# A new hand-written order for a recurrent attention layer with an MLP behind it, and its first weight loaded in three parts

## The chip, the cores and the metric

The kernel runs on one core of a Trainium2 chip. The time is the device time of one execution in microseconds (us): the median of three runs, of one core. A core has five engines that run side by side, each through its own instructions in their order: TensorE (PE in the profile; its weight loads are PEld), VectorE (DVE), ScalarE (ACT), GpSimd (POOL) and SyncE (SP), which here only issues transfers. Transfers run on 16 DMA engines. An instruction starts when those ahead of it on its engine and those whose results it needs are done.

## The reference

Four batches of eight heads, 768 steps, 48 numbers to a head. A state of 48x48 to a batch and head is carried from step to step, and its output goes through a two-layer MLP with a piecewise activation:

```python
for t in range(S):
    cur = einsum('bhd,bhe->bhde', u[None] * kt, vt)
    y[:, :, t] = einsum('bhd,bhde->bhe', rt, state + cur)
    state = w[None, :, :, None] * state + einsum('bhd,bhe->bhde', kt, vt)
x = y.transpose(0, 2, 1, 3).reshape(3072, 384)
h = x @ w_in                        # w_in: 384 x 2048
g = where(h >= 1, h, where(h <= -1, 0, (h + 1)**2 / 4))
out = g @ w_out                     # w_out: 2048 x 384
```

## The kernel before

**Tiles.** The 768 steps are cut into 6 chunks of 128, the 4 batches into 2 pairs. One chunk of one pair is a *group* g = 0 to 11 (g = 2 x chunk + pair); one chunk of one batch is a *unit* n = 2g or 2g+1. In a chunk the recurrence becomes matrix products: K and R are scaled by powers of w (`Ks`, `Rs`), turned (`T` and `TT` on TensorE for groups 0 to 2, `KRT`, a transposing transfer, from group 3 on), multiplied (`A`) and masked (`AT`); `Sp` is the chunk's addition to the state, `Tm`, `decay` and `sbf` carry the state on, `Y` is the output of a unit. The term with u goes beside it: `KU`, `RKU`, `usum` make one number to a row and head, `V2` multiplies V with it, and `y` adds that to `Y`. `X` and `xT` turn y: by TensorE and a copy for groups 0 to 2, by a transposing transfer (`xT` on SP's queue, tile `xT<-yy`) from group 3 on; `xT.8` is the one for group 4. V itself is cast to bf16 in step `V` (from tile `VF`).

**The MLP.** For group g and quarter q of the 2048 columns, `mm1.g.q` makes 512 columns of h for 256 rows (12 matmuls, line 526; in group 0 the first two quarters go in two halves), `relu` and `square` on ScalarE and `gate` on VectorE make the activation, and `mm2.g.j.q` (line 554, 4 matmuls) adds a quarter to the output of unit j. `o` copies it out of PSUM, `out` stores it. PSUM has three large buffers (h0 to h2), shared by `T`, `A` and the results of `mm1`, and two small banks.

**Weights.** `w_in` and `w_out` are loaded from f32 to bf16 by transfers that GpSimd issues (lines 290 and 294), in parts: `w_in.i`, `w_out.i`. Part i of `w_out` holds quarter i.

**The order.** It is written out by hand: `ORDER` is a list of steps, and each engine gets its instructions in the order of that list. A step is `name.numbers:buffers@engine`; `@D`, `@P`, `@A` put it on VectorE, GpSimd or ScalarE. `~k` puts k products of zeros ahead of a step, and `warm.k` is k of them (lines 204 and 608): they compute nothing. [...]

Of the kernel before, what the change touches and what calls it, by code (L numbers as in the profile page):

```python
# [14 lines left out]
P = 128  # L15
# [8 lines left out]
W_IN = 2  # L24
# [11 lines left out]
warm.18 load.K.0.0:0 load.R.0.0:0 load.K.0.1 load.R.0.1 load.K.1.0:1 load.R.1.0:1 bcu:0 u_bc@D KU.0.0@P:0 RKU.0.0@P:0  # L36
lw loadV.0.0:0 bcw:1 load.K.1.1 KU.0.1@D loadV.0.1 wcol:0 Wdn_p:0 Ks.0.0@D:0 Wup_p load.R.1.1 Rs.0.0@D:0 wCm
KU.1.0@P:1 loadV.1.0:1 Ks.1.0@D:1 warm.4.h.2 T.0:1 load.K.2.0:2 Wdn RKU.1.0@P:1 Rs.1.0@D:1 Rs.0.1@D V.0.0@A:0
RKU.0.1@P T.2:2~3 TT.0@A:0 usum.0.0@D:0 Ks.1.1@D Ks.0.1@D KU.1.1@P Wup Sp.0:0 TT.2@D:1 A.0:1 V.0.1@A load.R.2.0:2
AT.0.1:0 RKU.1.1@P Tm.0@D Sp.1:1~5 T.1:2 Tm.1@D w_in.0 V.1.0@A:1 A.2:1 Rs.1.1@D loadV.1.1 Sp.2:0 AT.0.0 TT.1@D:2  # L40
usum.1.0@A:1 A.1:0~8 V2.0.0@P:0 Ks.2.0@P:2 AT.2.0:1 loadV.2.0:0 V2.1.0@A:1 Y.0:1 T.3:2 sbf.0@A Tm.2@D usum.0.1@D Y.2:0
TT.3@D:3 y.2:0 AT.1.1:2 Rs.2.0@P:2 A.3:1~14 X.2:0 V2.0.1@A y.0:1 AT.3.0:3 warm.2.h.2 X.0:1 T.5:2~8 AT.1.0 xT.2@A:0
T.4:0 TT.5@D:0 Y.1:0 w_in.1 load.K.3.0:0 xT.0@A:1 sbf.1@A usum.1.1@D A.5:1 mm1.0.0.0:2 KU.2.0@P:0 y.1:2 TT.4@D:1
load.R.3.0:0 V.1.1@A X.1:1 Y.3:0 AT.5.0:0 A.4:0 V2.1.1@P xT.1@A mm1.0.0.1 V.2.0@A:2 Sp.5:1 y.3:0 RKU.2.0@P:0
relu.0.0:0 X.3:0 Tm.5@D:0 mm1.0.1.0:1 AT.4.0:1 xT.3@A decay.5 square.0.0:0 usum.2.0@D:0 Sp.4:1 mm1.0.1.1 w_out.0 Y.4:0
relu.0.1:1 mm1.1.1.-1:0 gate.0.0:0 square.0.1:1 Tm.4@D:1 mm1.0.2.-1:2 relu.1.1:0 Y.5:1 square.1.1:0 V2.2.0@P:0 w_out.1
y.4:1 gate.0.1:1 w_out.2 X.4:0 w_out.3 mm1.0.3.-1:1 xT.4@A:2 gate.1.1:2 relu.0.2:1 Sp.3:0 y.5:2 mm1.1.0.-1:0
# [56 lines left out]
def kernel(  # L104
# [33 lines left out]
    def flat(x):  # L138
# [24 lines left out]
        out=umask, in_=umask, compare_op=ALU.is_ge, fill=1.0,  # L163
# [486 lines left out]
```

## Time and profile before

| | |
|---|---|
| runs | 175.46, 175.96, 178.86 us; median 175.96 |
| profiled execution | span 176.4 us; the page gives no other time of it |
| busy in it | PE 165.0, ACT 135.2, DVE 130.3, POOL 120.2 us |
| granted clock of TensorE over the span | 0.987 |
| products of zeros | 24 (line 608) and 38 (line 204) |

Idle time of an engine costs only where something late waits for it. A busy PE is not PE at its peak; TensorE's own rate is seen in the durations of single steps and in the granted clock (PEclk, 1.00 is full).

### The profile page before, as it was taken

How to read it: one execution, taken by the hardware profiler on the slowest of the kernel's cores; microseconds unless marked ns; L12 is line 12 of the kernel's file. 1: busy time of each engine (PE TensorE's matmuls, PEld its weight loads, DVE VectorE, ACT ScalarE, POOL GpSimd, SP SyncE). 2: the span in 40 equal slices, each digit the busy share in tenths (PEclk: the TensorE clock that was granted, in tenths of full speed). 3: DMA queues.
4: the chain of work that ended last, by engine and by line, in shares of the span. 5: the costliest groups of instructions: out<-in, count | busy, mean ns of one | idle time of the engine just before them, and what ended most of it. 6: DMA issues, size and time to landing. Idle time of an engine off the chain costs nothing.

```text
span 176.4 us, 4159 instructions
## 1 busy us (share of the span) xinstructions
PE 165.0 (94%) x1684; PEld 125.2 (71%) x1684; DVE 130.3 (74%) x167; ACT 135.2 (77%) x194; POOL 120.2 (68%) x97
## 2 busy tenths in 40 slices
PE   6998699999999999779999999999999999999992
PEld 5776587766787766458686777885878767777671
DVE  5599779857987578727978889788895877461471
ACT  4399879996987995319989697989399994888540
POOL 6699999990899999999399799999349400000000
PEclk9999999999999999969999999999999999999998
DMA  5999999999999999996999997989982400312022
GB/s 109 221 219 192 216 175 234 207 165 209 238 172 196 191 202 252 158 183 175 196 221 211 185 183 159 266 149 243 194 197 93 89 17 4 97 37 89 4 89 89
DMA packets 106967, 28.78 MB, mean 163 GB/s; under 512 B 100930, under 2 KB 106180, under 8 KB 106948
## 3 DMA queue, kind: packets, MB, share of 16 engines
q1 hardware_dynamic: 103888, 25.24, 73.6%
q0 software_dynamic: 2912, 3.15, 11.4%
q8 instruction: 13, 0.21, 0.5%
q10 hardware_dynamic: 148, 0.13, 0.2%
q14 instruction: 6, 0.05, 0.1%
HBM read 20.45 MB, written 4.72 MB: 143 GB/s over the span
## 4 chain that ended last, share of the span: by engine, by line
PE 71%; DMA 13%; DVE 7%; ACT 5%; POOL 1%; issue 1%; DVEq 0%; POOLq 0%
PE hp L526 31%; PE op L554 30%; DMA VF<-in_v_dram 5%; DMA w_out_sb<-in_moe_w_out_dram 4%; DMA xT<-yy 3%; DVE AT L421 3%; PE A L406 2%; PE Y L446 2%; PE Y L441 2%; PE Sp L432 1%; ACT V L212 1%; PE ub L242 1%; POOL V L369 1%; PE wb L237 1%; ACT RKU L355 1%; DVE yy L468 1%
## 5 line engine op out<-in xcount | busy, mean ns | idle before, releaser
L526 PE MATMUL hp<-xT,w_in_sb 128*128 128x256 bf16 (+1 forms) x600 | 72.0, 271 | 3.4 <-DMA xT<-yy 2.2
L554 PE MATMUL op<-w_out_sb,gt 128*128 128x384 bf16 (+2 forms) x400 | 71.9, 320 | 0.1
L544 DVE SCALAR_TENSOR_TENSOR gt<-sq,hp 128x1024 bf16<-128x1024 f32 x48 | 57.9, 1216 | 16.2 <-ACT sq L539 16.1
L526 PEld LDWEIGHTS <-w_in_sb 128*128 128x128 bf16 x600 | 56.2, 99 | 13.9 <-issue 3.1
L534 ACT ACTIVATE pt<-hp 128x1024 f32<-128x1024 f32 x48 | 48.7, 1018 | 17.7 <-PE hp L526 17.4
L539 ACT ACTIVATE sq<-pt 128x1024 f32<-128x1024 f32 x48 | 50.4, 1057 | 1.2
L554 PEld LDWEIGHTS <-gt 128*128 128x128 bf16 x400 | 36.5, 98 | 19.3 <-issue 0.5
L421 DVE TENSOR_TENSOR AT<-A,umask 128x1024 bf16<-128x1024 f32 x22 | 26.5, 1218 | 2.2 <-PE A L406 1.9
L337 POOL TENSOR_TENSOR KU<-K,u_bc 128x768 f32<-128x768 f32 (+1 forms) x13 | 21.6, 1658 | 2.0 <-DVE u_bc L212 2.0
L344 POOL TENSOR_TENSOR RKU<-R,KU 128x768 f32<-128x768 f32 (+1 forms) x14 | 22.2, 1589 | 0.3
L489 POOL TENSOR_TENSOR state<-Tm,wCm 128x384 f32<-128x384 f32 x16 | 16.0, 1003 | 8.8 <-DVE Tm L476 8.6
L369 POOL TENSOR_TENSOR V<-V,diag 128x768 f32<-128x768 bf16 (+1 forms) x12 | 16.4, 1365 | 7.1 <-ACT V L212 4.7
L327 POOL TENSOR_TENSOR Ks<-Wdn,K 128x768 bf16<-128x768 f32 x10 | 18.2, 1818 | 1.2 <-DMA K<-in_k_dram 1.2
L327 POOL TENSOR_TENSOR Rs<-Wup,R 128x768 bf16<-128x768 f32 x10 | 18.2, 1819 | 0.1
L476 DVE TENSOR_TENSOR Tm<-Sp,state 128x384 f32<-128x384 f32 x16 | 8.9, 555 | 7.3 <-POOL Ks L327 3.4
L468 DVE TENSOR_TENSOR yy<-Y,V 128x384 bf16<-128x384 f32 x18 | 9.9, 554 | 5.0 <-PE Y L446 3.5
L212 ACT CAST V<-VF 128x768 bf16<-128x768 f32 (+1 forms) x14 | 10.2, 737 | 3.6 <-DMA VF<-in_v_dram 3.5
L446 PE MATMUL Y<-V,AT 128*128 128x48 bf16 x192 | 11.4, 185 | 1.2 <-POOL AT L416 0.9
L446 PEld LDWEIGHTS <-AT 128*128 128x128 bf16 x192 | 9.8, 98 | 2.8 <-POOL AT L416 1.3
L357 DVE TENSOR_REDUCE diag<-RKU 128x16 f32<-128x768 f32 (+1 forms) x13 | 11.1, 852 | 0.9 <-POOL RKU L344 0.9
L212 ACT COPY oo<-op 128x384 f32<-128x384 f32 x13 | 6.2, 476 | 6.7 <-PE op L554 6.3
L212 ACT CAST state_bf<-state 128x384 bf16<-128x384 f32 x20 | 10.0, 503 | 0.0
(77 smaller groups left out, 127.2 us busy)
## 6 DMA issues: line engine op xcount, KB each, us to landing
out_dram<-oo SPq DMA_DIRECT2D x11, 384.0 KB, 3.7
K<-in_k_dram SPq DMA_DIRECT2D x10, 384.0 KB, 4.8
R<-in_r_dram SPq DMA_DIRECT2D x10, 384.0 KB, 4.9
VF<-in_v_dram SPq DMA_DIRECT2D x10, 384.0 KB, 5.8
w_in_sb<-in_moe_w_in_dram POOLq DMA_DIRECT2D x2, 768.0 KB, 8.6
w_out_sb<-in_moe_w_out_dram POOLq DMA_DIRECT2D x4, 384.0 KB, 7.5
K<-in_k_dram SPq DMA_DIRECT2D x4, 192.0 KB, 3.8
R<-in_r_dram SPq DMA_DIRECT2D x4, 192.0 KB, 3.7
```

The costliest lines, as they stand in the source:

```text
L212: nc.scalar.copy(out, in_) if e == "A" else engines[e].tensor_copy(out, in_)
L327: engines[e].tensor_mul(of_unit(dst, j0, j1)[:, :, :, :D], rep(tab, j1 - j0), of_unit(tiles[what, g], j0, j1))
L337: engines[e].tensor_mul(of_unit(tiles["KU", g], j0, j1), of_unit(tiles["K", g], j0, j1), rep(u_bc, j1 - j0))
L344: engines[e].tensor_mul(of_unit(tiles["RKU", g], j0, j1), of_unit(tiles["R", g], j0, j1), of_unit(tiles["KU", g], j0, j1))
L369: engines[e].tensor_mul(tiles["V2", g][:, hs, :], tiles["V", g][:, hs, :], tiles["diag", g][:, hs].unsqueeze(2).to_broadcast([P, hs.stop - ...
L421: nc.vector.tensor_mul(t.rearrange("p i n t -> p (i n) t"), tiles.pop(("A", n)).rearrange("p i n t -> p (i n) t"), umask.unsqueeze(1).to_b ...
L446: nc.tensor.matmul(t[:, 2 * p + i, :], tiles["AT", n][:, i, p, :], tiles["V", g][:, j * H + 2 * p + i, :], start=(c == 0), stop=True, skip ...
L526: nc.tensor.matmul(hp[:, f, cols], w_in_sb[:, i, n0 : n0 + P], tiles["xT", g][:, units, i, :], start=(i == 0), stop=(i == nK - 1), skip_gr ...
L534: nc.scalar.activation(tiles["pt", g, q], tiles["hp", g, q], AF.Relu, bias=0.5, scale=0.5)
L539: nc.scalar.activation(tiles["sq", g, q], tiles.pop(("pt", g, q)), AF.Square, bias=0.0)
L544: nc.vector.scalar_tensor_tensor(out=gt, in0=tiles.pop(("sq", g, q)), scalar=1.0, in1=tiles.pop(("hp", g, q)), op0=ALU.min, op1=ALU.max)
L554: nc.tensor.matmul(t, tiles["gt", g, q][:, f, j * P : (j + 1) * P], w_out_sb[:, n, cols], start=(n == 0), stop=(n == nF - 1),)
```

## The change

`w_in` comes in three parts: columns 0 to 511 (quarter 0), 512 to 1023 (quarter 1) and 1024 to 2047 (quarters 2 and 3). The order is another one throughout, with the same computation. Of the steps with a free choice of engine, VectorE takes 3 more of `KU`, 6 more of `RKU`, 1 of `Ks`, 2 of `Rs`, 6 of `V`, 8 of `sbf`, 3 of `xT`, one of `usum` and one of `V2`, and gives up 4 of `TT`, 4 of `o` and `u_bc`. GpSimd loses what VectorE gains of `KU`, `RKU`, `Ks`, `Rs`; two whole-group `V2` go from GpSimd to ScalarE. The products of zeros go from 62 to 42.

```diff
-W_IN = 2
+W_IN = (0, 512, 1024, 2048)
...
-warm.18 load.K.0.0:0 load.R.0.0:0 load.K.0.1 load.R.0.1 load.K.1.0:1 load.R.1.0:1 bcu:0 u_bc@D KU.0.0@P:0 RKU.0.0@P:0
+load.K.1.0:1 loadV.1.0:1 lw warm.2.h.2 bcw:1 bcu:0 V.1.0@A:4 Wdn_p:2 load.K.0.0:0 load.R.0.0:0 Wup_p Wup u_bc@A
...
     def w_in_go(e, bk, i):
-        n = slice(i * DF // W_IN, (i + 1) * DF // W_IN)
+        n = slice(W_IN[i], W_IN[i + 1])
         nc.gpsimd.dma_start(out=w_in_sb[:, :, n], in_=w_in_src[:, :, n])
```

**GpSimd, from its first `KU` to the second part of w_in.** Before (`V_327<-V,diag` is a half `V2`; `AT<-AT` is the mask of a first unit; x384 is half a group, 16x48 or 768 a whole one):

```order
L337 TENSOR_TENSOR KU<-K,u_bc 128x384
L344 TENSOR_TENSOR RKU<-R,KU 128x384
L290 DMA w_in_sb<-in_moe_w_in_dram 128x3x1024
L416 AFFINE_SELECT AT<-AT 128x1024
L369 TENSOR_TENSOR V_327<-V,diag 128x384
L327 TENSOR_TENSOR Ks<-Wdn,K 128x16x48
L327 TENSOR_TENSOR Rs<-Wup,R 128x16x48
L416 AFFINE_SELECT AT<-AT 128x1024
L290 DMA w_in_sb<-in_moe_w_in_dram 128x3x1024
```

After:

```order
L369 TENSOR_TENSOR V_239<-V,diag 128x384
L369 TENSOR_TENSOR V_274<-V,diag 128x384
L416 AFFINE_SELECT AT<-AT 128x1024
L344 TENSOR_TENSOR RKU<-R,KU 128x384
L290 DMA w_in_sb<-in_moe_w_in_dram 128x3x512
L327 TENSOR_TENSOR Rs<-Wup,R 128x16x48
L290 DMA w_in_sb<-in_moe_w_in_dram 128x3x512
L416 AFFINE_SELECT AT<-AT 128x1024
L290 DMA w_in_sb<-in_moe_w_in_dram 128x3x1024
L294 DMA w_out_sb<-in_moe_w_out_dram 128x4x384
```

Ahead of the first part of w_in stood seven halves of `KU` and `RKU`, now five (the rows shown begin behind the first four of them); two half `V2` and a mask have moved ahead of it, and the first part of w_out follows right behind the last part of w_in.

**SP, the transfers ahead of `xT.8`** (the row `xT<-yy`; KT and RT are `KRT`, `out_dram<-oo` is `out`). Before:

```order
L304 DMA VF<-in_v_dram 128x16x48
L304 DMA R<-in_r_dram 128x16x48
L304 DMA VF<-in_v_dram 128x16x48
L398 DMA_TRANSPOSE RT<-Rs 128x8x128
L587 DMA out_dram<-oo 128x2x384
L304 DMA K<-in_k_dram 128x16x48
L511 DMA_TRANSPOSE xT<-yy 128x6x128
```

After:

```order
L398 DMA_TRANSPOSE KT<-Ks 128x8x128 x2
L398 DMA_TRANSPOSE RT<-Rs 128x8x128
L304 DMA R<-in_r_dram 128x16x48
L304 DMA VF<-in_v_dram 128x16x48
L304 DMA K<-in_k_dram 128x16x48
L511 DMA_TRANSPOSE xT<-yy 128x6x128
```

A store and a transpose no longer stand among the four transfers ahead of it.

**VectorE, the gates of groups 2 and 3** (`gt<-sq,hp` is `gate`, `diag<-RKU` is `usum`, `yy<-Y` is `y`). Before:

```order
L544 SCALAR_TENSOR_TENSOR gt<-sq,hp 128x1024 x2
L212 COPY oo<-op 128x384
L544 SCALAR_TENSOR_TENSOR gt<-sq,hp 128x1024 x2
L357 TENSOR_REDUCE diag<-RKU 128x16
L544 SCALAR_TENSOR_TENSOR gt<-sq,hp 128x1024 x2
L421 TENSOR_TENSOR AT<-A,umask 128x1024 x2
```

After:

```order
L544 SCALAR_TENSOR_TENSOR gt<-sq,hp 128x1024
L337 TENSOR_TENSOR KU<-K,u_bc 128x768 x2
L544 SCALAR_TENSOR_TENSOR gt<-sq,hp 128x1024
L344 TENSOR_TENSOR RKU<-R,KU 128x768
L544 SCALAR_TENSOR_TENSOR gt<-sq,hp 128x1024
L212 CAST V<-VF 128x768
L357 TENSOR_REDUCE diag<-RKU 128x16
L544 SCALAR_TENSOR_TENSOR gt<-sq,hp 128x1024
L327 TENSOR_TENSOR Rs<-Wup,R 128x16x48
```

Between the gates now stand `KU.4`, `KU.5`, `RKU.4`, `V.4` and `Rs.5`, which were GpSimd's and ScalarE's, and which need loads of K, R and V.

On TensorE the steps from `mm1.0.2` (the first that needs columns from 1024 on) up to `mm1.4.0` (the first that needs `xT.8`) are the same set in both kernels but for `Y.5`, which now stands ahead of `mm1.0.2`. Behind the second `Y` of group 4 there were a quarter of `mm2`, two `A` and four more quarters with two `Sp` among them; now there are two `A`, four quarters and two `Sp`.

126 lines of the change are left out of this document (63 added, 63 removed).

## The prediction

> **What bounds the kernel now.** I read the engines' shares first, then the span by stretches, then the chain that ended last. The shares:
>
> ```profile
> PE 165.0 (94%) x1684; PEld 125.2 (71%) x1684; DVE 130.3 (74%) x167; ACT 135.2 (77%) x194; POOL 120.2 (68%) x97
> DMA  5999999999999999996999997989982400312022
> ```
>
> TensorE leads by 30 us, and the DMA engines are full for the first three quarters of the span. Where TensorE is not full shows in the stretches (busy us of PE, PEld, DVE, ACT, POOL, then PEclk, DMA share, GB/s):
>
> ```profile
> 22.00:31.00 9.00, 8.15 (x129) 7.08 (x130) 7.80 (x10) 7.75 (x10) 8.68 (x9) 1.00 1.19 205
> 31.00:64.00 33.00, 32.84 (x296) 24.71 (x292) 24.51 (x28) 29.30 (x37) 28.04 (x20) 1.00 1.20 196
> 64.00:76.00 12.00, 9.61 (x106) 5.87 (x105) 10.05 (x12) 5.74 (x9) 11.55 (x9) 1.00 1.24 193
> 76.00:80.00 4.00, 3.94 (x33) 3.15 (x33) 0.79 (x2) 1.15 (x2) 4.00 (x3) 0.57 1.08 212
> 80.00:100.00 20.00, 19.61 (x212) 15.03 (x210) 17.00 (x20) 18.04 (x21) 16.03 (x11) 1.00 0.95 203
> 100.00:160.00 60.00, 60.00 (x615) 45.93 (x613) 46.99 (x52) 49.19 (x59) 33.08 (x22) 1.00 0.62 131
> ```
>
> From 31 on TensorE works without a gap but for one hole, 64 to 76, and runs at a clock of 0.57 for 4 us behind it. Another order can win there at most the 2.4 us idle in that stretch, 4 x (1 - 0.57) = 1.7 us of clock, and 0.39 us idle in 80 to 100: 4.5 us. All else must come from the head, before 31. The chain names what both wait for:
>
> ```profile
> 14.46 9.60 DMA VF<-in_v_dram
> 30.26 7.92 DMA w_out_sb<-in_moe_w_out_dram
> 69.89 6.13 DMA xT<-yy
> 76.06 2.72 PE hp L526 x12
> ```
>
> In the head these are transfers of V and of the weights; in the hole it is `xT.8`, which landed 6.1 us after its issue. TensorE's own rows at the two places (start, duration, in brackets the idle time before):
>
> ```profile
> 29.18 1.48 PE L526 MATMUL hp<-xT,w_in_sb 128*128 128x256 bf16 x12 [0.29 <-DMA w_in_sb<-in_moe_w_in_dram]
> 73.07 0.81 PE L554 MATMUL op<-w_out_sb,gt 128*128 128x384 bf16 x4
> 76.06 2.72 PE L526 MATMUL hp<-xT,w_in_sb 128*128 128x256 bf16 x12 [2.18 <-DMA xT<-yy]
> 79.54 1.47 PE L526 MATMUL hp<-xT,w_in_sb 128*128 128x256 bf16 x12
> ```
>
> `mm1.0.2` starts at 29.18, when the second half of w_in lands. The last quarter of group 3 ends at 73.88, and `mm1.4.0` starts at 76.06, at half speed (2.72 us; 1.47 at 79.54). Between those two steps TensorE hardly pauses, so a delay of `mm1.0.2` is carried to 73.88 whole.
>
> **The change, part by part. First the weights.** When does GpSimd issue them?
>
> ```profile
> 3.55 1.62 PE L242 MATMUL ub<-u_row,ones 97*128 97x384 f32 x2 [0.40 <-DVE wCm L179]
> 13.26 0.93 POOL L290 DMA_DIRECT2D w_in_sb<-in_moe_w_in_dram  x1
> 26.91 0.80 POOL L294 DMA_DIRECT2D w_out_sb<-in_moe_w_out_dram  x1
> L246 ACT ACTIVATE Wup<-wb,up_col 128x384 f32<-128x384 f32 x1 | 0.6, 592 | 0.0
> L344 POOL TENSOR_TENSOR RKU<-R,KU 128x384 f32<-128x384 f32 x4 | 4.0, 998 | 0.2
> L369 POOL TENSOR_TENSOR V<-V,diag 128x384 f32<-128x384 bf16 x2 | 1.7, 836 | 0.0
> L416 POOL TENSOR_SCALAR_AFFINE_SELECT AT<-AT 128x1024 bf16<-128x1024 bf16 x2 | 2.2, 1101 | 0.0
> L327 POOL TENSOR_TENSOR Rs<-Wup,R 128x768 bf16<-128x768 f32 x10 | 18.2, 1819 | 0.1
> ```
>
> GpSimd's first `KU` waits for `u_bc`. Now `bcw` takes the first place on TensorE (from about 3.55 to 5.2), ScalarE makes three tables and then `u_bc`, four steps of 0.5 to 0.6: `KU.0.0` starts near 7.4. Ahead of w_in stand five halves of `KU` and `RKU` (1.0 each), two half `V2` (0.84) and a mask (1.10): 7.8 us, so not before 15.2. The second `V2` waits for a `usum` behind ten or so steps of VectorE, which adds up to 1.6. I take 16.0 (15.2 to 16.8) against 13.26. The last part follows behind `Rs.2` (1.82), a mask and two issues of 0.87: 16.0 + 4.7 = 20.7. How long the data takes:
>
> ```profile
> w_in_sb<-in_moe_w_in_dram POOLq DMA_DIRECT2D x1, 768.0 KB, 8.7
> w_out_sb<-in_moe_w_out_dram POOLq DMA_DIRECT2D x1, 384.0 KB, 7.0
> ```
>
> The first half of w_in took 8.7 us beside the loads on SP's queue. Both in a row at that pace: 16.0 + 17.4 = 33.4. The other end: w_out's first part, issued at 26.91, landed at 33.9, and its third at 38.2 (30.26 + 7.92 in the chain), so 768 KB in 4.3 us once few loads were open; with 4.3 for quarter 0 the last columns would land at 16.0 + 4.3 + 6.4 = 26.7. The latest is 16.0 + 7.0 + 13.0 = 36.0, with w_out's 7.0 for quarter 0. The loads of K, V, R of groups 2 and 3 stand beside the weights now as then, so I stay near the first figure and take 32.5. **Term 1: +3.3** (0 to +6.6; not below nothing, since VectorE's and GpSimd's steps ahead of the first gates are no fewer). Nothing covers this wait but `Y.5`, now done before it (12 small products, priced near the eight of an `A`, 0.35 below): **term 2: -0.4**. w_out's parts then land every 2.2 us from about 34.7, and TensorE wants the first only after three and more `mm1` of 1.31, at 36.8: no wait there.
>
> **The hole.** TensorE runs out of work at 73.88 + 3.3 - 0.4 = 76.8. Behind the second `Y` of group 4 stand four quarters, two `A` and two `Sp`. Below, the chain's rows for a quarter, an `mm1`, an `A` and an `Sp`; SP's rows ahead of `xT.8` (it was issued at 69.89); and the landing times of the nine `xT`:
>
> ```profile
> 46.95 0.65 PE op L554 x4
> 47.60 1.31 PE hp L526 x12
> 82.69 0.35 PE A L406 x8
> 45.30 0.17 PE Sp L432 x4
> 67.59 0.57 SPq L587 DMA_DIRECT2D out_dram<-oo  x1
> 68.21 0.46 SPq L304 DMA_DIRECT2D K<-in_k_dram  x1
> DMA to landing us min/median/max: 2.7/2.8/6.1
> ```
>
> That is 2.6 + 0.7 + 0.3 = 3.6 us, so this `Y` ends at 73.2, its `y` (0.57) at 73.8, and `xT.8` lands at 76.6 with the median 2.8, or at 79.9 with the 6.1 it had. It had 6.1 because a store and a K load were put on the queue 2.3 and 1.7 us ahead of it; now the loads R.6, V.6 and K.7 precede. V.6 and K.7 only wait for the cast `V.5`, which stands behind `relu.3.3` and ends about when `A.8` starts; from there to `xT.8` TensorE has two `A`, six quarters and two `Y`, some 5.4 us, in which these loads drain. I take 2.8: no wait, `mm1.4.0` at 76.8, 0.7 later than before (**term 3: +0.7 in place of terms 1 and 2**), and without the hole no slow clock: **term 4: -1.7** (0 to -1.7).
>
> **VectorE's new work.** What the trace has of it:
>
> ```profile
> L337 DVE TENSOR_TENSOR KU<-K,u_bc 128x384 f32<-128x384 f32 x1 | 0.6, 559 | 0.0
> L357 DVE TENSOR_REDUCE diag<-RKU 128x16 f32<-128x768 f32 x10 | 9.4, 945 | 0.9 <-POOL RKU L344 0.9
> L212 DVE COPY TT<-T 128x1024 bf16<-128x1024 bf16 x5 | 3.4, 684 | 1.1 <-PE T L388 1.1
> ```
>
> A whole-group product is not among them: between 0.56 and 1.12 (one half, two halves), nearest the reduce over the same 768 numbers, 0.95. Ten of these (`KU`, `RKU`, `Ks`, `Rs`) 9.5; four halves 2.2; `V` 4 x 0.95 + 2 x 0.56 = 4.9; `sbf` 8 x 0.56 = 4.5; `xT` 1.7; less `TT` 2.7 and five copies (`o`, `u_bc`) 2.8: +17.3, to 148 of 176 us. GpSimd loses 23 us and ScalarE hardly changes. The most crowded place is between the last `mm2` of group 0 and the last of group 3: VectorE then has 10 gates 12.2 (1.22 each), 6 `AT` at the same 7.3, 9 `Tm` and `y` 5.0, 3 `usum` 2.8, six moved products and casts 5.7, 4 copies 2.2: 35.2; TensorE has 24 quarters 15.6, 8 `mm1` 10.5, 6 `A` 2.1, the rest 2.6: 30.8. Before, VectorE had 24.5 of 33 us busy in 31 to 64, so much of it slips into gaps; GpSimd's relief can't win, as no wait on it is left on TensorE there. After 80, **term 5: +0.3** (-0.4 to +5).
>
> The Trainium skill's "VectorE: DVE Perf Modes" (section "The perf-mode tier table (the rule you actually need)") lets an f32 copy inside SBUF run at twice the rate of a two-input product. By it the six casts of `V` would cost, as an estimate, about 2 us less. No row here shows such a cast on VectorE.
>
> **Sum:** 176.4 + 0.7 - 1.7 + 0.3 = 175.7 against the profiled span. The span is 0.4 above the median of the runs, so 175.3 against 175.96.
>
> **Rivals.** *A, the weights come early.* `mm1.0.2` at 29.2 as before, TensorE out of work at 73.5, `xT.8` (73.5 - 3.6 + 0.6 + 2.8 = 73.3) in time: 176.4 - 2.6 - 1.7 + 0.3 = 172.4, 172.0 by the median. For it: w_out's pace; quarter 0 alone is half the bytes. Against: the DMA row full of nines up to 130, and the later issue.
>
> *B, VectorE sets the pace: slower.* A step is late when VectorE waits for a load ahead of a gate, or has more to do than TensorE beside it. In the crowded stretch 35.2 - 30.8 = 4.4 us; in groups 5 and 7 I count some 2 more, so up to 6.4. `KU.4` is the place: `gate.2.1` and, behind it, the PSUM buffer of `mm1.3.1` wait for it.
>
> ```profile
> DMA to landing us min/median/max: 2.9/4.1/13.7
> L544 DVE SCALAR_TENSOR_TENSOR gt<-sq,hp 128x1024 bf16<-128x1024 f32 x48 | 57.9, 1216 | 16.2 <-ACT sq L539 16.1
> ```
>
> The first row is of the loads of K. VectorE's 16.1 us of waiting for squares are its reserve. It decides once more than about 1.5 us of the new work stands ahead of a due gate; 5 of the 6.4 us would give 180.3 by the median.
>
> *C, fewer products of zeros leave TensorE slow.*
>
> ```profile
> 8.19 0.63 PE L388 MATMUL T<-ident,Ks 128*128 128x128 bf16 x4
> 12.25 0.38 PE L388 MATMUL T<-ident,Ks 128*128 128x128 bf16 x4
> ```
>
> Four transposes took 0.63 us at 8.2 and 0.38 at 12.3: TensorE was slow up to about 11 us even with 24 products of zeros ahead. With 20 fewer it may stay so up to the first `mm1`: some 5 us of products between 12 and 22 take twice as long, of which the wait for w_in hides 3.3: 175.3 + 1.7 = 177.0. The Trainium skill's "TensorE: Matmul & The Clock Gate" (section "Part 1: The HAM clock gate (the "warmup" mystery)") says that throttled is the default and about 3.4 us of sustained work releases it; it speaks against dropping them. The 0.57 behind the hole agrees, though TensorE was wholly idle for only 2.2 us there.
>
> **How the numbers follow.** Chances: forecast 0.42, A 0.26, B 0.22, C 0.10. A measurement of this kernel can tell about 2%, 3.5 us, from no change. A lies at that bound and beyond and is counted as faster, with 0.02 of the forecast; B as slower, with 0.04 of the forecast (term 1 at its upper end with a 6 us `xT.8`). So faster 0.28, same 0.46, slower 0.26. The range takes in A and B: 171.5 to 181; the forecast's own is 173 to 178.
>
> **What would show it.** Right: w_in's last part issued near 21 and landing past 31, TensorE waiting 2 to 4 us on w_in at `mm1.0.2`, no wait over 1 us on `xT<-yy` near 77, PEclk 1.00 there, POOL near 98 and DVE near 148 us busy. Wrong: `mm1.0.2` before 30 (A); TensorE waiting for VectorE's `gt` between 45 and 75, or idle reappearing after 100 (B); the transposes still at 0.6 past 15 us (C).

## The result, and the profile after

The changed kernel takes **186.58 us** (median of 185.94 to 187.18) beside 176.01 for the kernel before on the same chip: a ratio of 1.062, 95% interval 1.057 to 1.068. It is slower by 6%, where 175.3 was forecast. Every execution's time is 1.7 us above its span; the profiled one of the changed kernel has a span of 184.7. The ratios below leave disturbed executions out and the medians do not, so kernels are compared by their ratios to the kernel before, which ran beside each of them (174.4 to 175.3 us).

The engines' shares of the changed kernel, then the same stretches as before (busy us of PE, PEld, DVE, ACT, POOL, then PEclk, DMA share, GB/s):

```profile
PE 164.6 (89%) x1664; PEld 123.9 (67%) x1664; DVE 157.3 (85%) x189; ACT 136.0 (74%) x194; POOL 100.0 (54%) x84
```

```profile
22.00:31.00 9.00, 7.30 (x140) 6.55 (x137) 8.60 (x10) 7.26 (x11) 6.43 (x6) 1.00 1.18 193
31.00:64.00 33.00, 29.97 (x283) 23.04 (x281) 29.07 (x31) 25.41 (x30) 19.85 (x14) 0.98 1.02 177
64.00:76.00 12.00, 12.00 (x103) 8.08 (x101) 11.87 (x13) 9.55 (x12) 6.95 (x5) 0.91 0.93 203
76.00:80.00 4.00, 4.00 (x51) 2.76 (x51) 4.00 (x6) 3.12 (x13) 3.92 (x3) 1.00 0.67 129
80.00:100.00 20.00, 17.55 (x202) 14.01 (x201) 19.34 (x23) 16.00 (x22) 18.53 (x13) 1.00 0.96 192
100.00:160.00 60.00, 57.47 (x586) 42.79 (x584) 55.39 (x60) 47.42 (x68) 29.49 (x21) 1.00 0.67 141
```

TensorE's hole from 64 to 76 is gone, but it is now idle where it was full: 3.0 us between 31 and 64, 2.45 between 80 and 100, 2.5 after that. In these stretches it is VectorE that is nearly full: 29.1 of 33 us, 19.3 of 20 and 55.4 of 60. GpSimd is at 100 us, as the prediction had it (98); VectorE is at 157.3, not 148. The shares of the chain that ended last, then its pieces (start, duration) about `gate.2.1` and TensorE's row behind them:

```profile
PE 54%; DVE 29%; issue 9%; ACT 7%; ACTq 0%; DVEq 0%
```

```profile
55.49 0.70 DVE gt L544
56.19 0.43 issue
56.62 2.47 DVE KU L337 x2
59.09 2.33 issue
61.42 1.22 DVE gt L544
```

```profile
62.68 4.45 PE L526 MATMUL hp<-xT,w_in_sb 128*128 128x256 bf16 x24 [2.94 <-DVE gt L544]
```

No DMA is in the chain any more, and VectorE holds 29% of it. The place that rival B named is in it: `KU.4` and `KU.5` stand between two gates and take 4.8 us from 56.62 to 61.42, priced at 1.9; TensorE waits 2.94 us for the gate, and its next 24 products, which begin with `mm1.3.1`, take 4.45 us (2.78 for as many at 32.75, below), with a granted clock of 0.91 in 64 to 76. The groups of VectorE (busy us, mean ns | idle before them) show what grew dearer:

```profile
L544 DVE SCALAR_TENSOR_TENSOR gt<-sq,hp 128x1024 bf16<-128x1024 f32 x48 | 58.1, 1215 | 13.7 <-ACT sq L539 12.9 <-PE op L554 0.4
L212 DVE CAST state_bf<-state 128x384 bf16<-128x384 f32 x8 | 8.9, 1112 | 0.0
L337 DVE TENSOR_TENSOR KU<-K,u_bc 128x768 f32<-128x768 f32 x3 | 6.8, 2282 | 0.0
L344 DVE TENSOR_TENSOR RKU<-R,KU 128x768 f32<-128x768 f32 x4 | 5.1, 1280 | 0.0
```

The gates, which read PSUM, take what they took (1216 before). The moved products were priced at 0.95 us and take 2.28 and 1.28; the moved casts of `sbf` were priced at 0.56 and take 1.11.

The head is late too. The rows of TensorE at `mm1.0.2` and at `mm1.4.0`, and of the weight load, whose last part was issued at 22.5 (the last line is the time to landing of the three parts):

```profile
32.75 2.78 PE L526 MATMUL hp<-xT,w_in_sb 128*128 128x256 bf16 x24
80.62 1.47 PE L526 MATMUL hp<-xT,w_in_sb 128*128 128x256 bf16 x12
```

```profile
L290 POOL DMA_DIRECT2D w_in_sb<-in_moe_w_in_dram x3: 778/804/925, 17.5 to 22.5; - x3
DMA to landing us min/median/max: 6.0/6.9/7.7
```

`mm1.0.2` starts at 32.75 as forecast (32.5; 29.18 before), but its row names no wait for `w_in`: at the longest, 7.7 us from 22.5, the last part is there at 30.2. Something else makes the head late. In the chain it is VectorE, from 6.37 to 17.35 without a break but for 1.07 us, and again from 23.6 to 27.9; two of its rows there:

```profile
8.78 2.65 DVE L344 TENSOR_TENSOR RKU<-R,KU 128x384 f32<-128x384 f32 x2
24.16 2.14 DVE L369 TENSOR_TENSOR V<-V,diag 128x384 f32<-128x384 bf16 x1
```

These are `RKU.0.0` with `RKU.1.0`, and the half `V2.1.1`, all three new on VectorE. A half was priced at some 0.56; they take 1.36 and 2.14 each. Behind the `V2` stands a `y` for which TensorE waits 0.99 us at 27.96. The moved steps are thus dearer in the head as well; whether they are what makes it late is tried below.

### The profile page after: what moved, and what is told of

Its sections match the earlier page's. It is cut to its first block, busy times and chain, and to the rows that moved or that the text cites. A ratio compares the mean times of both kernels' runs of the same rounds, so it can differ in the third digit from the quotient of the medians.

```text
span 184.7 us, 4142 instructions
## 1 busy us (share of the span) xinstructions
PE 164.6 (89%) x1664; PEld 123.9 (67%) x1664; DVE 157.3 (85%) x189; ACT 136.0 (74%) x194; POOL 100.0 (54%) x84
## 4 chain that ended last, share of the span: by engine, by line
PE 54%; DVE 29%; issue 9%; ACT 7%; ACTq 0%; DVEq 0%
PE hp L526 24%; PE op L554 20%; DVE gt L544 7%; DVE AT L421 6%; ACT sq L539 3%; DVE KU L337 3%; ACT pt L534 2%; PE A L406 2%; DVE Tm L476 2%; DVE yy L468 2%; DVE diag L357 2%; PE Y L446 2%; DVE V L212 2%; PE Y L441 1%; DVE V L369 1%
## 5 line engine op out<-in xcount | busy, mean ns | idle before, releaser
L554 PE MATMUL op<-w_out_sb,gt 128*128 128x384 bf16 (+2 forms) x400 | 69.7, 320 | 2.0 <-DVE gt L544 1.4
L369 POOL TENSOR_TENSOR V<-V,diag 128x768 f32<-128x768 bf16 (+1 forms) x10 | 13.5, 1349 | 34.1 <-DVE diag L357 16.8
L489 POOL TENSOR_TENSOR state<-Tm,wCm 128x384 f32<-128x384 f32 x16 | 16.5, 1036 | 7.8 <-DVE Tm L476 7.8
L327 POOL TENSOR_TENSOR Ks<-Wdn,K 128x768 bf16<-128x768 f32 x9 | 16.7, 1856 | 3.7 <-DMA K<-in_k_dram 2.3
L337 POOL TENSOR_TENSOR KU<-K,u_bc 128x768 f32<-128x768 f32 (+1 forms) x10 | 15.7, 1570 | 4.5 <-ACT u_bc L212 3.4
L344 POOL TENSOR_TENSOR RKU<-R,KU 128x768 f32<-128x768 f32 (+1 forms) x8 | 13.2, 1647 | 6.0 <-DVE diag L357 5.8
L327 POOL TENSOR_TENSOR Rs<-Wup,R 128x768 bf16<-128x768 f32 x8 | 15.3, 1908 | 1.2 <-DMA R<-in_r_dram 1.2
L212 ACT COPY oo<-op 128x384 f32<-128x384 f32 x16 | 7.5, 472 | 6.4 <-PE op L554 5.4
L367 ACT ACTIVATE V<-V,diag 128x48 f32<-128x48 bf16 x40 | 9.3, 320 | 0.1
L212 DVE CAST state_bf<-state 128x384 bf16<-128x384 f32 x8 | 8.9, 1112 | 0.0
```

What stands on the lines that cost most here:

```text
L212: nc.scalar.copy(out, in_) if e == "A" else engines[e].tensor_copy(out, in_)
L327: engines[e].tensor_mul(of_unit(dst, j0, j1)[:, :, :, :D], rep(tab, j1 - j0), of_unit(tiles[what, g], j0, j1))
L337: engines[e].tensor_mul(of_unit(tiles["KU", g], j0, j1), of_unit(tiles["K", g], j0, j1), rep(u_bc, j1 - j0))
L369: engines[e].tensor_mul(tiles["V2", g][:, hs, :], tiles["V", g][:, hs, :], tiles["diag", g][:, hs].unsqueeze(2).to_broadcast([P, hs.stop - ...
L489: nc.gpsimd.tensor_mul(states[(g % BP) * UNITS + j], tiles.pop(("Tm", n)), wCm)
L554: nc.tensor.matmul(t, tiles["gt", g, q][:, f, j * P : (j + 1) * P], w_out_sb[:, n, cols], start=(n == 0), stop=(n == nF - 1),)
```

## Experiments

**Theories.** 1: VectorE sets the pace, since the moved steps are many and take longer beside GpSimd than alone. 2: the order of the steps (the late head, the weights, the transfers) makes the lag. 3: fewer products of zeros leave TensorE's clock slow.

| kernel | ratio to before, 95% interval |
|---|---|
| the changed kernel | 1.062, 1.057 to 1.068 |
| e1: nine products back on GpSimd | 1.043, 1.039 to 1.047 |
| e2: twelve casts back on ScalarE | 1.039, 1.035 to 1.043 |
| e3: both back | 1.030, 1.025 to 1.035 |
| e4: before, with both moved | 1.043, 1.032 to 1.053 |
| e5: before, with w_in in three parts | 1.000, 0.998 to 1.003 |
| e6: changed, 16 products of GpSimd left out | 1.016, 1.012 to 1.021 |
| e13: changed, these products as memsets | 1.031, 1.023 to 1.039 |
| e7: changed, 23 more products of zeros | 1.053, 1.044 to 1.061 |

### Two engines, and what they share

A kernel of its own runs VectorE's kinds of operations eight at a time, first alone, then beside GpSimd:

```diff
+phases = [("mul", 8, "mul", 0), ("cast", 8, "mul", 0), ..., ("mul", 0, "mul", 6), ...
+    ("mul", 8, "mul", 8), ("cast", 8, "mul", 8), ("red", 8, "mul", 4), ("gate", 8, "mul", 5), ...
+    ("mul", 8, "asel", 8), ("mul", 8, "set", 8)]   # VectorE's kind, count, GpSimd's kind, count
```

> A kernel of its own that computes nothing of the reference: on each of 18 stages VectorE does 8 operations of one kind, alone or while GpSimd does operations of its own, and nothing else runs. Theory 1 (the two engines exclude each other where a VectorE operation reads two operands from SBUF or casts inside SBUF): alone, a product of 128x768 f32 takes 0.95 us, a cast 0.55, a cast of 128x384 0.35, the reduce 0.95, the gate 1.22; beside GpSimd's products of 1.82 us the product takes about 1.9 to 2.8, the cast 1.8 to 2.4, the small cast 1.8 to 2.2, while the reduce, the gate (one operand from PSUM) and the copies and sums from PSUM stay within 3% of alone. Theory 2 (the longer durations are the DMA's or the whole machine's, not GpSimd's): every kind takes the same with and without GpSimd beside it.

VectorE's rows in time order (start, duration of the eight together): alone first, then the same beside GpSimd's products; the last two rows are its products beside GpSimd's `affine_select`, which reads SBUF, and those that were to run beside memsets, which read nothing. Below them GpSimd's memsets, its six products alone and its eight beside VectorE's eight.

```profile
5.14 7.91 DVE L44 TENSOR_TENSOR dmul<-go,other 128x768 f32<-128x768 f32 x8 [5.14 <-ACT other L31]
13.32 4.72 DVE L45 CAST cast<-go 128x768 bf16<-128x768 f32 x8 [0.27 <-ACT go L75]
18.38 3.12 DVE L46 CAST scast<-go 128x384 bf16<-128x384 f32 x8 [0.33 <-ACT go L75]
21.82 7.87 DVE L47 TENSOR_REDUCE red<-go 128x16 f32<-128x768 f32 x8 [0.32 <-ACT go L75]
31.58 10.01 DVE L48 SCALAR_TENSOR_TENSOR gt<-sq,big 128x1024 bf16<-128x1024 f32 x8 [1.89 <-ACT big L81]
...
77.88 18.27 DVE L44 TENSOR_TENSOR dmul<-go,other 128x768 f32<-128x768 f32 x8 [23.11 <-ACT other L80]
98.59 13.60 DVE L45 CAST cast<-go 128x768 bf16<-128x768 f32 x8 [2.43 <-ACT go L78]
116.10 10.55 DVE L46 CAST scast<-go 128x384 bf16<-128x384 f32 x8 [3.91 <-ACT go L78]
132.45 7.87 DVE L47 TENSOR_REDUCE red<-go 128x16 f32<-128x768 f32 x8 [5.80 <-ACT go L78]
143.04 10.01 DVE L48 SCALAR_TENSOR_TENSOR gt<-sq,big 128x1024 bf16<-128x1024 f32 x8 [2.72 <-ACT big L81]
...
168.42 12.52 DVE L44 TENSOR_TENSOR dmul<-go,other 128x768 f32<-128x768 f32 x8 [1.74 <-ACT other L80]
184.19 7.91 DVE L44 TENSOR_TENSOR dmul<-go,other 128x768 f32<-128x768 f32 x8 [3.25 <-ACT other L80]
```

```profile
1.69 6.31 POOL L58 MEMSET pset<- 128x768 f32 x8
56.01 11.20 POOL L54 TENSOR_TENSOR pmul<-go,other 128x768 f32<-128x768 f32 x6 [48.01 <-ACT other L80]
77.93 19.88 POOL L54 TENSOR_TENSOR pmul<-go,other 128x768 f32<-128x768 f32 x8 [1.18 <-ACT other L80]
```

Beside GpSimd's products a product on VectorE goes from 0.99 to 2.28 us, a cast from 0.59 to 1.70, a small cast from 0.39 to 1.32. The reduce and the gate do not change by 0.01 us in eight, nor do a copy and a sum that read PSUM (4.70 us for eight of either, in both cases). Beside `affine_select` a product takes 1.57. GpSimd pays as well, 2.49 in place of 1.87. The stage with the memsets failed: they wait for nothing and all ran from 1.69 us on, so the row at 184.19 is a second one of VectorE alone, and what a memset does is seen in e13 only. That the two engines hold each other up is shown, and 2.28 is also the mean of `KU` in the changed kernel; the casts came out below the expected 1.8.

The Trainium skill's "SBUF — State Buffer" (section "Who interferes with whom") has this as a lock on a port pair that VectorE and GpSimd share: a VectorE instruction with two SBUF inputs meets GpSimd instructions that read SBUF, a copy or cast in its two-port mode meets any, a reduce none. The rows above agree; none of them has a GpSimd instruction that only writes. It says that the loser blocks for the whole instruction; here a pair of products takes 2.49 us and not the 0.99 + 1.87 = 2.86 of both alone.

### Does it matter in the kernel?

Two runs take the sharing away and leave VectorE its steps: e6 drops GpSimd's products, e13 keeps GpSimd busy with instructions that read nothing.

```diff
 def scaled(e, bk, g, j, what):
+    if e == "P" and g >= 3:
+        return                                          # e6
+        for _ in range(3): nc.gpsimd.memset(dst, 0.0)    # e13, in place of the return
     engines[e].tensor_mul(...)
```

> The changed kernel without those products Ks and Rs that stand on GpSimd for groups 3 to 11 (their tiles keep older values; some 14 products of 1.8 us are left out, 26 us of GpSimd's 100). VectorE's steps are those of the changed kernel. Theory 1a (VectorE's work is dear because it waits for GpSimd's products): KU on VectorE falls from 2.28 to below 1.6 us, sbf from 1.11 to below 0.8, VectorE to 145 to 151 us busy, and the time by 2 to 5 us to 181.5 to 184.5. Theory 1b (the work alone is too much): the durations stay within 10%, the time within 1 us of 186.6.

> The changed kernel, with each product Ks and Rs of groups 3 to 11 that stands on GpSimd replaced by three memsets of the same tile (about 0.7 us each, 2.1 in place of 1.86; the products are left out of the result). GpSimd is as busy as in the changed kernel or busier, but these instructions read nothing from SBUF. Theory 1a (VectorE's instructions wait for GpSimd's where both read SBUF; the run without these products gave 177.9): KU on VectorE below 1.2 us, VectorE at 146 to 150 us busy, 177 to 180. Theory 1c (GpSimd being busy, or what waits for it, is what costs): within 1.5 us of 186.6.

Of e6, then of e13, VectorE's group of `KU` and that of `sbf`:

```profile
L339 DVE TENSOR_TENSOR KU<-K,u_bc 128x768 f32<-128x768 f32 x3 | 2.8, 948 | 0.0
L212 DVE CAST state_bf<-state 128x384 bf16<-128x384 f32 x8 | 6.1, 766 | 0.0
```

```profile
L341 DVE TENSOR_TENSOR KU<-K,u_bc 128x768 f32<-128x768 f32 x3 | 2.8, 946 | 0.0
L212 DVE CAST state_bf<-state 128x384 bf16<-128x384 f32 x8 | 9.3, 1165 | 0.0
```

e6: VectorE 147.6 us busy and 177.87 us, by the ratios some 8 below the changed kernel, more than the 2 to 5 expected. It drops 16 products of GpSimd's (the expectation said some 14), and what follows from them is earlier as well, so not all of that is sharing. e13 is the cleaner one: GpSimd is busier than in the changed kernel (106.2 us), and `KU` is back at its lone 0.95, two of the three wholly beside memsets. The casts of `sbf` do not come back; GpSimd's remaining products and its decay steps stand beside them as well as memsets, and the run does not part these. The time is 180.95, 5.6 below, a little above the expected 177 to 180, as is VectorE with 151.8 us. Theory 1c falls. e13 leaves the moved steps on VectorE and comes to 1.031, no worse than e3 below, where they are put back (1.030): that speaks for the sharing and against the mere number of steps. It is no proof, since a memset also does not wait for the loads of K and R, as GpSimd's products did for 3.5 us.

### Undoing the moves, and doing them alone

```diff
 # e1, and e3 with e2
-KU.4.0@D KU.5.0@D KU.9.0@D RKU.4.0@D RKU.9.0@D RKU.10.0@D RKU.11.0@D Rs.3.0@D Rs.5.0@D
+KU.4.0@P KU.5.0@P KU.9.0@P RKU.4.0@P RKU.9.0@P RKU.10.0@P RKU.11.0@P Rs.3.0@P Rs.5.0@P
 # e2, and e3 with e1
-V.4.0@D V.6.0@D V.9.0@D V.11.0@D sbf.2@D sbf.4@D sbf.6@D sbf.8@D ... sbf.11@D sbf.19@D
+V.4.0@A V.6.0@A V.9.0@A V.11.0@A sbf.2@A sbf.4@A sbf.6@A sbf.8@A ... sbf.11@A sbf.19@A
```

> The changed kernel with nine products of groups 3 to 11 back on GpSimd (KU.4, KU.5, KU.9, RKU.4, RKU.9, RKU.10, RKU.11, Rs.3, Rs.5). Theory 1 (VectorE's new work sets the pace between 55 and 130 us, and it is dearer than predicted since it waits for GpSimd): VectorE loses 14.6 us of 157.3, the middle loses over half of its 9.6 us of idle TensorE and slow clock, 178 to 182. Theory 2 (the lag comes from the late head and from the order of the steps and transfers, not from the engines): 185 to 187. Theory 3 (clock, fewer products of zeros): 185 to 187.

> The changed kernel with twelve casts of groups 1 to 11 back on ScalarE (V of groups 4, 6, 9, 11 and sbf of units 2, 4, 6, 8, 9, 10, 11, 19). Theory 1 (VectorE sets the pace): VectorE loses 12.5 us of 157.3 and the products that stay on it have the same long durations; 179 to 183. Theory 2 (head and order) and theory 3 (clock): 185 to 187; if ScalarE, which gets some 7 us more, is late instead, above that.

> The changed kernel with both the nine products and the twelve casts back on the engines that they had before, so that only the order, the weights and the head's engines are the changed ones. Theory 1 (VectorE sets the pace): VectorE at about 130 us busy, no idle of TensorE over 1 us between 55 and 130 us but for late loads, 175 to 178. Theory 2 (head and order): 183 to 187, with mm1.4.0 still about 8 us later than before. Theory 3 (clock): 184 to 187.

Medians 182.89, 182.10 and 180.90 us. Each half gives back 3 to 4 us by the ratios, both 5.7; theories 2 and 3 expected at least 183 for e3. e1 ends just above theory 1's 178 to 182: it falls short of VectorE's relief because GpSimd is late in its turn; VectorE's row of `usum.4` in e1:

```profile
64.93 0.95 DVE L357 TENSOR_REDUCE diag<-RKU 128x16 f32<-128x768 f32 x1 [3.49 <-POOL RKU L344]
```

The gates of group 3 stand behind that reduce. e3 stays 3% above the kernel before, above theory 1's range: VectorE is not the whole cause. The other way round, the same 21 steps moved in the order of before (e4), and that order with the three parts of w_in alone (e5):

```diff
-W_IN = 2
+W_IN = (0, 512, 1024, 2048)
-... Tm.1@D w_in.0 V.1.0@A:1 ... Y.1:0 w_in.1 load.K.3.0:0 ...
+... Tm.1@D w_in.0 w_in.1 V.1.0@A:1 ... Y.1:0 w_in.2 load.K.3.0:0 ...
```

> The kernel before, in its own order, with the nine products and twelve casts of groups 1 to 11 put on VectorE (the same steps that the runs above put back). Theory 1 (VectorE's new work sets the pace, whatever the order): VectorE goes from 130 to 152 to 158 us busy, the products on it take 1.3 to 2.4 us and the casts of sbf over 0.9 us each; 179 to 183 against 175.3. Theory 2 (the order is what costs): 174.5 to 177.

> The kernel before with w_in in three parts, the second issued right behind the first and the third where the second half stood; nothing else is changed. Theory 1 (the weights are not what costs): 174.5 to 176.5, mm1.0.2 within 1 us of where it was. Theory 2 in the form that the weights make the late head: mm1.0.2 starts 2 us or more later, 177 or above.

e4: 182.52 us, +7.5, with this trace of its `KU` and `Rs` on VectorE:

```profile
L327 DVE TENSOR_TENSOR Rs<-Wup,R 128x768 bf16<-128x768 f32 x2 | 4.9, 2461 | 0.0
L337 DVE TENSOR_TENSOR KU<-K,u_bc 128x768 f32<-128x768 f32 x3 | 4.8, 1610 | 0.0
```

So the moves alone, in an order that had nothing else changed, cost no less than the changed kernel gives back without them (7.5 and 5.7 us; the interval of e4 holds both). Not all went as expected: VectorE is 150.4 us busy in place of 152 to 158, and the casts of `sbf` take 0.65 us in place of over 0.9, so there the products carry the price. e5: 175.03, no change; the parts of w_in are not the cause. e5 is also a second trace of the old order, and it speaks of the hole:

```profile
64.00:76.00 12.00, 11.94 (x140) 8.02 (x138) 10.56 (x12) 6.88 (x12) 11.54 (x9) 1.00 1.17 227
76.00:80.00 4.00, 3.86 (x49) 3.08 (x46) 3.14 (x6) 3.94 (x5) 3.97 (x4) 1.00 0.87 162
```

TensorE has no hole here and no slow clock, though SP has the same store and K load ahead of `xT.8`, 2.8 and 2.1 us earlier: it lands 3.2 us after its issue, not 6.1. The spans of the 45 further executions of the kernel before, beside the runs, are 172.1 to 175.5 us, the profiled one's 176.4.

### The clock, and the hole by itself

```diff
-... lw warm.2.h.2 bcw:1 ... load.K.0.1 warm.2.h.1 load.R.0.1 ...   # e7
+... lw warm.20.h.2 bcw:1 ... load.K.0.1 warm.6.h.1 load.R.0.1 ...
-... AT.8.0:0 out.0 decay.8 mm2.2.1.3 load.K.7.0:1 mm2.3.0.1 ... xT.8:0 o.3.0@A:0 ...   # e8, in the order of before
+... AT.8.0:0 decay.8 mm2.2.1.3 mm2.3.0.1 ... xT.8:0 load.K.7.0:1 out.0 o.3.0@A:0 ...
```

> The changed kernel with 23 more products of zeros in the head (20 and 6 in place of 2 and 1), so that it has as many as the kernel before or more. Theory 3 (fewer of them leave TensorE slow, and this costs): the transposes from 8 us on take 0.38 per four, and the time falls by 1 us or more, to 183.5 to 185.5. Theories 1 and 2: the clock may change in the first 22 us, the time stays at 186 to 187, since the head waits for VectorE and ScalarE.

> The kernel before with the load of K of group 7 and the store of group 0 put on the queue behind xT.8 in place of ahead of it; nothing else is changed. If the hole at 64 to 76 us and the slow clock behind it are in every execution, as the prediction took it (2.2 us of waiting and 1.7 of clock): 171.0 to 172.5. If they were in the profiled execution alone (the spans of other executions of the kernel before are 172.8 to 174.2 us, and with w_in in three parts the trace has no such hole): 174.2 to 175.5.

e7 gives 183.67, which theory 3 had expected, but not by its route: the transposes still take 0.59 to 0.63 us per four up to 17.5 us, and `mm1.0.2` starts at 32.22, 0.5 earlier. By the ratios the gain is not clear of the noise (1.053 and 1.062, with intervals that overlap; the fourth execution took 186.20). In the two traces it begins at 54 us. The changed kernel there, VectorE and then GpSimd:

```profile
53.88 1.69 DVE L212 CAST state_bf<-state 128x384 bf16<-128x384 f32 x1
...
56.62 4.88 DVE L337 TENSOR_TENSOR KU<-K,u_bc 128x768 f32<-128x768 f32 x2
...
53.54 1.81 POOL L327 TENSOR_TENSOR Ks<-Wdn,K 128x768 bf16<-128x768 f32 x1 [2.25 <-DMA K<-in_k_dram]
```

And e7:

```profile
53.67 0.35 DVE L212 CAST state_bf<-state 128x384 bf16<-128x384 f32 x1
...
55.07 3.26 DVE L337 TENSOR_TENSOR KU<-K,u_bc 128x768 f32<-128x768 f32 x2
...
54.01 1.82 POOL L327 TENSOR_TENSOR Ks<-Wdn,K 128x768 bf16<-128x768 f32 x1 [2.93 <-DMA K<-in_k_dram]
```

In the changed kernel GpSimd's `Ks.4` starts 0.34 us ahead of `sbf.4`, which waits it out; in e7 it starts 0.34 us behind, when the cast is done. Who comes first makes 1.3 us for the cast, and the two `KU` behind it take 1.6 less. That is where the trace of e7 wins; no run tried it apart. e8 failed as an experiment, 182.25 us: the store moved behind `xT.8` also frees a buffer, and ScalarE's copy `o` waits for it,

```profile
76.33 0.48 ACT L212 COPY oo<-op 128x384 f32<-128x384 f32 x1 [6.50 <-DMA out_dram<-oo]
```

so it says nothing on the hole. e5 does.

### What remains: the head

After e3 some 5.3 us (1.030) remain. Where the kept traces lose time, by the starts of two steps and the span (`mm1.0.2` of e5 stands in a row of 24 products from 27.31 on):

| trace | `mm1.0.2` | `mm1.4.0` | span |
|---|---|---|---|
| e5: the order of before | about 28.9 | 74.04 | 173.2 |
| e4: the moves alone | 28.96 | 77.00 | 179.4 |
| e3: the changed order, moves put back | 31.97 | 78.02 | 177.6 |
| the changed kernel | 32.75 | 80.62 | 184.7 |

In e3's trace, its fastest execution, `mm1.0.2` is 3.1 us later than in e5, `mm1.4.0` 4.0 and the end 4.4: most of the remainder is there when `mm1.0.2` starts, and nothing behind it takes it back. In e4 the head is on time and all is lost behind it.

Besides the order e3 keeps sixteen steps of the head on other engines, and behind the head copies (`o`, `xT`) and two `V2`. First seven of the sixteen were put back, then the zeros as well:

```diff
-KU.1.0@D RKU.0.0@D RKU.1.0@D Ks.2.0@D V2.1.1@D V.0.0@D V.0.1@D   # e9, on top of e3
+KU.1.0@P RKU.0.0@P RKU.1.0@P Ks.2.0@P V2.1.1@P V.0.0@A V.0.1@A   # e10: and the zeros of e7
```

> The run with the products and casts of the steady part put back (180.9 us), with those of the head put back too: KU.1.0, RKU.0.0, RKU.1.0, Ks.2 and the half V2.1.1 on GpSimd, the two halves of V.0 on ScalarE. Theory 1 for the head (VectorE, without idle from 6 to 28 us and with two RKU of 1.3 us, a Ks of 1.8 and a V2 of 1.9 that wait for GpSimd, makes mm1.0.2 late): mm1.0.2 starts 1.5 us or more earlier than its 32, and the time is 177 to 179.5. Theory 2 (the order of the head or its clock makes it late): mm1.0.2 stays within 0.7 us and the time at 180 to 182.

> The run before this one (all engines put back) with 23 more products of zeros in the head. Theory 3 (fewer of them leave TensorE slow and this is what remains): 1 us or more below that run. Otherwise within 0.7 us of it: the 2.9 us that they gave in the changed kernel came from VectorE's and GpSimd's steps falling otherwise, not from the clock.

No gain: 1.033 (1.029 to 1.038) and 1.044 (1.037 to 1.051). In e10, `mm1.0.2` is later, not earlier:

```profile
32.94 2.78 PE L526 MATMUL hp<-xT,w_in_sb 128*128 128x256 bf16 x24 [0.21 <-DVE gt L544]
```

GpSimd, with five more products in the head, issues the last part of w_in 2.3 us later (23.99 for 21.70 in e3). Its chain to `mm1.0.2` leads back from the gate over a `usum` to GpSimd's `RKU.2`, which starts at 28.94 (25.86 in e3). One late engine took the place of another, so the two runs show that the head isn't won by these seven steps or by zeros, and not that VectorE has no part in it. Next the order: the steps ahead of `mm1.0.2` are nearly the same set in both kernels (the changed one has also `Y.5`, `V2.2`, a gate and three parts of w_out there), so they were put in the order of before, on its engines and with its zeros, under e3's remainder (e11) and under the changed one (e12); then with the PSUM buffers renumbered (e14, e15); then with w_out issued right behind w_in (e16, e17).

```diff
-load.K.1.0:1 loadV.1.0:1 lw warm.2.h.2 bcw:1 ... w_out.3 square.1.1:0 y.5:2 mm1.0.2.-1:0 ...
+warm.18 load.K.0.0:0 load.R.0.0:0 ... gate.0.1:1 w_out.2 w_out.3 y.5:2 mm1.0.2.-1:0 ...   # e11, e12
+... mm1.0.0.0:0 ... mm1.0.1.0:2 ... mm1.1.1.-1:1 ... (were :2, :1, :0)                    # e14, e15
+... Y.1:0 w_in.2 w_out.0 w_out.1 w_out.2 w_out.3 load.K.3.0:0 ...                         # e16, e17
```

> The run with the products and casts of the steady part put back (180.9 us), and with the steps ahead of mm1.0.2 in the order and on the engines of the kernel before, its products of zeros included; from mm1.0.2 on the changed order. If the head's order is what remains: mm1.0.2 starts near 29.2 in place of 32, the first gate at 27.5 to 28, and the time is 176.5 to 178.5. If what remains is the order behind the head: 180 to 182.

> The changed kernel with the steps ahead of mm1.0.2 in the order and on the engines of the kernel before; from mm1.0.2 on all is the changed kernel, its moved products and casts too. If the two causes add up (VectorE's steady work 5.7 us, the head 3.3 us): 182 to 184. If VectorE alone sets the end, a head that is 3 us earlier is lost again: 185 to 187.

> The run with the head's order and the steady part's engines put back, whose seam made mm1.0.2 wait 2.9 us for a gate of the same PSUM buffer; here the three large PSUM buffers of the head are renumbered (0 as 1, 1 as 2, 2 as 0), so that mm1.0.2 and mm1.0.3 find the buffers that they had in the kernel before. If the head's order makes what remains of the 5.7 us: mm1.0.2 near 29.5, 176 to 178.5. If it does not: 180 to 182.

> The changed kernel with the head's order and engines of the kernel before and the same renumbered buffers; from mm1.0.2 on all is the changed kernel. If the two causes add up: 182 to 184. If VectorE alone sets the end, the head's 3 us are lost again: 185 to 187.

> The run with the head's order, its buffers and the steady part's engines put back (182.1 us, where TensorE waited 1.1 and 3.7 us for parts of w_out), with the four parts of w_out issued right behind the last part of w_in. If the head's 3 us were lost to w_out: no wait on w_out, 177 to 179.5. If what remains is the order behind the head: 180.5 to 182.5 without that wait.

> The changed kernel with the head of the kernel before (184.6 us, 1.9 us of waiting for w_out) and w_out issued right behind w_in. If head and VectorE add up: 182.5 to 183.7, 3 to 4 below the changed kernel. If the wait for w_out only gives way to VectorE's: 184 to 185.5.

Ratios: e11 1.048, e12 1.055, e14 1.039, e15 1.057, e16 1.052, e17 1.067. None fulfils an expectation of a head that adds up, and most lie outside both ranges given. e11 and e12 have a wait of 2.9 us at the seam of the two orders, where `mm1.0.2` and a gate not yet done share a buffer. e15 is the telling one:

```profile
29.82 2.78 PE L525 MATMUL hp<-xT,w_in_sb 128*128 128x256 bf16 x24
...
39.47 0.81 PE L553 MATMUL op<-w_out_sb,gt 128*128 128x384 bf16 x4 [1.92 <-DMA w_out_sb<-in_moe_w_out_dram]
```

`mm1.0.2` is 2.9 us earlier, so the order, the engines and the zeros of the head, taken together, are what makes it late; 1.9 of these are lost again to `w_out`, and by the ratios 0.9 reaches the end (1.057 beside 1.062, with intervals that overlap). Taking that wait away (e16, e17) puts a `V2` on GpSimd behind the four issues, which take 3.0 us, and TensorE waits 2.8 us for the `y` that needs it. Which steps of the new head cost the remaining 5.3 us stays open: each transplanted head got a new wait from what stands behind it. No version came out below the kernel before.

## Why the prediction was wrong

- **Term 5, VectorE's new work, is the step that failed.** Its counts were right and most of its prices were not. "A whole-group product, nearest the reduce, 0.95" took the price from rows where nothing was shared: alone it is 0.95, in the changed kernel beside GpSimd 2.28 (`KU`) and 1.28 (`RKU`) on average; `sbf` 1.11 for 0.56. The casts of `V` came out as priced (0.90 for 0.95) by luck: alone they take 0.55 to 0.59, and the sharing made up the rest. The new work came to 157.3 - 130.3 = 27.0 us for 17.3, and its effect on the time to 5.7 us by e3 and 7.5 by e4, where the sum had 0.3 with an upper end of 5. The nearest row was the reduce, a kind that does not share. The trace of before did hold a sign of it, where both engines make a half `KU` at once and GpSimd's takes 1.36 (1.00 a little later):

```profile
5.80 0.56 DVE L337 TENSOR_TENSOR KU<-K,u_bc 128x384 f32<-128x384 f32 x1
...
5.85 1.36 POOL L337 TENSOR_TENSOR KU<-K,u_bc 128x384 f32<-128x384 f32 x1 [2.01 <-DVE u_bc L212]
```

- **Rival B was right in direction and place** (`KU.4` ahead of `gate.2.1` and `mm1.3.1`, TensorE waiting for `gt` between 45 and 75, idle reappearing after 100). Its 6.4 us at most lies beside the 5.7 to 7.5 that the moves cost, by luck in part: it was counted from the number of steps at their lone prices. It fell short of the whole 10.6 us since it has no late head beside it, and its chance was 0.22. "GpSimd's relief can't win" held; its busy time was right to 2 us.
- **Term 1: the size right by luck, the cause wrong.** `mm1.0.2` came at 32.75 for 32.5, without the wait on w_in that was to show it. w_in was issued later than forecast (22.5 for 20.7) and landed faster (7.7 us for its 768 KB). e5 shows that the three parts cost nothing, e15 that the head's order, engines and zeros do. Its own test, "waiting 2 to 4 us on w_in", is what caught it. (By the prediction's own 36.0 the upper end is +6.8, not +6.6; nothing hangs on it.)
- **Terms 3 and 4, the hole, priced one execution.** The wait on `xT.8` was gone, as forecast, but there was nothing to win: e5 has neither the 2.2 us nor the slow clock, and its `xT.8` lands in 3.2 us behind the same store and K load that were to explain the 6.1. Term 3 also let the hole swallow most of the late head, +0.7 in place of +2.9; without a hole to swallow it the 3.1 us stay, as the table of traces has it. The same slip is in "the span is 0.4 above the median": an execution's time is 1.7 us *above* its span, so the profiled one took some 178.1, and a gain that only it could have was taken off the median of all.
- **Rival C**: slow transposes up to 17.8 us came (0.61 to 0.63 from 14.2 on, though 0.38 at 9.1), as C said, and decided little. In e3, with the same head, the products of `A` are fast from 18.8 on (0.40 for eight; 0.61 up to 21.0 in the changed kernel), and `mm1.0.2` is only 0.8 us earlier. e7's zeros did not make the transposes faster, so e7 and e10 do not test C's price. In e5, with the zeros of before, four at 12.53 take 0.63 where the profiled execution of before had 0.38 at 12.25. The Trainium skill's "TensorE: Matmul & The Clock Gate" (section "Part 1: The HAM clock gate (the "warmup" mystery)") calls the number of slow products variable from run to run, and the two traces agree, though e5 has one issue more on GpSimd ahead of them.
- **Rival A** fell with the late head.

By what was measured: some 175.2 for a usual execution, 5.7 for the moves by e3 and the 5.3 that e3 leaves make 186.2, beside 186.6. That closes by construction; e4's 7.5 is the one independent figure, and with it the sum is 188.0. The second part is known by its size and only partly by its place.

## What to carry to other kernels

Price work that is moved to VectorE by rows where GpSimd is busy beside it: in these runs operations with two operands in SBUF, and casts inside SBUF, cost up to 2.6 times (a product, 2.46 us in e4 for 0.95) and 3.4 times (small casts) their lone duration, while reduces and operations with an operand in PSUM cost the same; those are the ones to move. Ask for a second trace, or the spans of other executions, before a hole in the first is counted as a gain. In an order written by hand, a step's buffer, queue place and engine are tied to what stands behind it, so a part that is taken over alone tends to bring a new wait.

## What the hardware showed that was not expected

- Beside GpSimd's products of 1.87 us a product of 128x768 f32 on VectorE takes 2.28 for 0.99, and GpSimd's 2.49: a pair takes 2.49, less than the 2.86 of both in turn.
- A GpSimd memset leaves VectorE's products alone (`KU` 946 ns in e13, 948 in e6 without any instruction in its place), while `sbf`, a cast, stays at 1165 ns in e13 (766 in e6).
- A start that differs by 0.7 us between the two engines (`Ks.4` 0.34 ahead of `sbf.4` or 0.34 behind) goes with a cast of 1.69 or 0.35 us, and the two kernels, 0.5 us apart at `mm1.0.2`, are 3.2 us apart at the next gate but one (61.4 and 58.2).
